# Last keys of the value product in 64-row tiles, one pool of PSUM banks, and engine orders from a table, in an attention kernel with a squared-ReLU feed-forward network

## The chip, the cores and the metric

The kernel runs on one core of one Trainium2 chip. The metric is the device time of one execution in microseconds (us). Engines are written as in the profile: PE is TensorE, DVE is VectorE, ACT is ScalarE, POOL is GpSimd, SP is SyncE; PEld is PE's loading of weights.

## The reference

Eight batches of eight heads, 576 positions, 64 dimensions a head. To the scores a bias is added that depends on the distance of two positions and on the head; then softmax, the product with the values, and a feed-forward network on the 4608 rows of 512:

```python
scores = scale * np.matmul(q, k.transpose(0, 1, 3, 2))
scores = scores + bias.transpose(2, 0, 1)[None, :, :, :]
attn = np.exp(scores - np.max(scores, axis=-1, keepdims=True))
attn = attn / (np.sum(attn, axis=-1, keepdims=True) + 1e-09)
attn_out = np.matmul(attn, v)
x = attn_out.transpose(0, 2, 1, 3).reshape(B * S, H * D)
h = np.maximum(x @ w_in, 0.0)        # w_in 512 x 2048
return h * h @ w_out                 # w_out 2048 x 512
```

## The kernel before, in words

**Attention.** The work goes by pairs of heads, 32 in all (`pair`, L919; four to a batch). Keys are laid on partitions, in four tiles of 128 and a last one of 64 (keys 512 to 575); queries run along the free dimension. Scores of the four full key tiles (`scores_of`, L807, matmul L815) use 64 rows of the array for each head, since a head has 64 dimensions: the two heads of a pair run as two 64-row tiles. They write to a set of two PSUM banks, one bank a head, and one exponential on ACT (L997, 1024 elements a partition) reads the set. The last 64 queries have products of their own (L822, 64 columns each, two banks) and two exponentials (L831, one a head). For the last 64 keys both heads share one full tile (`last_keys`, L1006): `kz` holds head 0's keys on one half of the rows and columns and head 1's on the other, so that one product (L1012) gives both heads' scores on 128 partitions; `pm` holds their exponentials (L1022). The bias enters as a factor: DVE multiplies the bands near the diagonal by a table of exponentials of the bias (L728, the "bands").

The product with the values (`values`, L741) goes over tiles of 128 queries: for each tile one product of the last keys of both heads at once (L754: `pm` against `vm`, which holds zeros where heads don't belong together, 130 columns) and eight of 65 columns (L761: four key tiles for two heads); the 65th column gives the sum of the softmax. A pair is done in two parts, of three and of two query tiles, each in one bank. DVE takes the reciprocal (L775) and writes the normalized rows `x` (L780). From batch 2 on a DMA transpose on SP turns `x` into `xt`, one for each part; for the first two batches PE does it (L1078). The first batch is done in halves of its queries (`half_of_pair`, L840).

**Feed-forward network.** It goes over nine groups of 512 rows, while the attention of later batches runs. The first layer is 16 products of 128 columns of `w_in` for a group (L1501; for group 0 by halves, L1451; part of the groups 2 to 8 by a scheme with seven products for eight, L1378). ACT applies the ReLU (L1530) and DVE squares (L1540) into `g`. The second layer uses seven products for eight as well (L1204), with sums of `g` made on DVE and evictions on DVE and ACT (L1232, L1238).

**Order.** All work is a list of operations with an engine or a choice of engines, what they depend on, and the buffers they take (`Plan.add`). `Plan.schedule` (L191) picks at each step the operation that can start first by a cost model, and among those the one that is due first. Due times come from the code and, for some 500 operations, from a table of numbers (`DUES`, L67). The instructions are then issued in that order, and each engine runs its own in order; semaphores make it wait. A buffer is taken from a ring of slots when the operation is placed. PSUM has two rings: two sets of two banks for scores (`sets_ps`, L347), and four single banks for all else (`g_ps`, L348). The loads of the start are issued by POOL; q and k of a pair go to buffers `qs` and `ks`, the weights in four pieces each.

Of the kernel before, what the change touches and what calls it, by code (L numbers as in the profile page):

```python
# [34 lines left out]
RELU_DVE = 0  # L35
# [31 lines left out]
DUES = """  # L67
# [52 lines left out]
"""  # L120
# [5 lines left out]
class Ring:  # L126


    def __init__(self, n, in_order=False):
        self.free = [(0.0, i) for i in range(n)]  # L130
        self.in_order, self.made, self.taken = in_order, 0, 0


class Buf:


    def __init__(self, ring):
        self.ring, self.left, self.slot, self.until = ring, 0, None, 0.0
        self.turn, ring.made = ring.made, ring.made + 1
# [31 lines left out]
STAY = 0.0  # L171


class Plan:
# [16 lines left out]
    def schedule(self):  # L191
        engines = ("PE", "ACT", "DVE", "POOL", "SP", "DMA", "XB")
        now = {"PE": 600.0, "ACT": 740.0, "DVE": 820.0, "POOL": 1300.0, "SP": 740.0, "DMA": 0.0, "XB": 0.0}
        mode = None
        waiting = {e: [] for e in engines}
        for op in self.ops:
            op.wait = len(op.deps)
            for d in op.deps:
                d.users.append(op)
            if not op.wait:  # L200
                for e in op.engs:
                    waiting[e].append(op)
        done = []
        while len(done) < len(self.ops):
            best = None
            for e in engines:
                pick = None
                for op in waiting[e]:
                    at = max(now[e], op.ready, self._buf_time(op))
                    if at == float("inf"):  # L210
                        continue
                    due = op.due if op.due > -1e8 else op.ready - 1e9
                    if e == "PE" and op.mode != mode:
                        due += STAY
                    key = (max(at, now[e]), due, op.seq)
                    if pick is None or key < pick[0]:
                        pick = (key, op)
                if pick is None:
                    continue
# [50 lines left out]
def act(n):  # L270
    return 174.0 + n / 1.2
# [1337 lines left out]
```

## Time and profile before

| what | us |
|---|---|
| three runs | 360.20, 360.44, 362.07 |
| their median | 360.44 |
| span of the profiled execution, first to last instruction | 358.7 |
| busy: PE, PEld | 346.4, 262.0 |
| busy: DVE, ACT, POOL | 297.5, 272.6, 170.6 |

Of the profiled execution the span is on record and not its time beside it; the median of the runs is 1.7 above the span, for what lies before the first instruction and behind the last. In the profile, a line such as L815 is a line of the kernel before. A row of PE's timeline gives the start, the length of the merged piece, the line, the output and inputs, the tile (128\*128 is the whole array, 64\*128 half of its rows), the shape, and the count. Matmuls are pipelined, so the length of one is longer than the distance between the starts of two.

### The profile page before, as it was taken

Reading aid. Unit: us, or ns where it says so; the run is one execution under the profiler, and the core shown is the slowest. Engines: PE = TensorE matmul, PEld = TensorE weight load, DVE = VectorE, ACT = ScalarE, POOL = GpSimd, SP = SyncE. Lnnn points to the kernel's source line nnn. Section 1 sums busy time; section 2 is a strip of 40 time slices with the busy share of each in tenths; the row PEclk is TensorE's granted clock in tenths of the full one; section 3 lists DMA queues with packets and bytes.
Section 4 is the critical chain, followed back from the end, with each engine's and each line's share of the span. In section 5 each row is a group of like instructions: output and inputs, shape, how many; then the busy total and the mean of one; then the engine's idle time right before and its main releaser. Section 6 shows DMA issues by size and latency. Waiting matters only on the chain.

```text
span 358.7 us, 10742 instructions
## 1 busy us (share of the span) xinstructions
PE 346.4 (97%) x4290; PEld 262.0 (73%) x4290; DVE 297.5 (83%) x673; ACT 272.6 (76%) x435; POOL 170.6 (48%) x289
## 2 busy tenths in 40 slices
PE   3988999999999999999999999999999999999996
PEld 3666788775587558877788568755867887888885
DVE  4888999666996799768896899798988798899993
ACT  4898997589966988678976887689889833899830
POOL 8886679698995896158478456221000000000000
PEclk9999999999999999999999999999999999999999
DMA  9999999999999999799999999863410032010023
GB/s 172 151 147 198 193 150 154 190 156 192 175 130 165 223 158 112 119 163 198 84 134 164 186 126 133 150 121 72 61 44 15 18 97 68 27 63 33 23 66 117
DMA packets 162210, 44.37 MB, mean 124 GB/s; under 512 B 145520, under 2 KB 162160, under 8 KB 162160
## 3 DMA queue, kind: packets, MB, share of 16 engines
q0 software_dynamic: 74208, 14.53, 54.6%
q1 hardware_dynamic: 87696, 28.86, 44.3%
q8 instruction: 33, 0.54, 0.6%
q10 hardware_dynamic: 256, 0.30, 0.3%
q14 instruction: 17, 0.14, 0.1%
HBM read 36.94 MB, written 9.44 MB: 129 GB/s over the span
## 4 chain that ended last, share of the span: by engine, by line
PE 88%; DMA 7%; POOL 2%; ACT 1%; issue 1%; DVE 0%; POOLq 0%
PE f L1204 31%; PE f L1501 20%; PE f L761 10%; PE st L815 8%; PE f L1378 7%; DMA w_in_sb<-in_moe_w_in_dram 5%; PE f L1451 3%; PE st L1378 3%; PE f L754 3%; PE st L1012 2%; DMA ks<-in_k_dram 2%; POOL va L368 2%; PE f L822 1%; PE f L1078 1%; POOL ks L368 0%
## 5 line engine op out<-in xcount | busy, mean ns | idle before, releaser
L997 ACT ACTIVATE pt<-st 128x1024 f16<-128x1024 f32 x112 | 111.1, 1031 | 23.0 <-PE st L815 22.8
L1501 PE MATMUL f<-xt,w_in_sb 128*128 128x512 f16 (+4 forms) x416 | 77.2, 330 | 0.0
L728 DVE TENSOR_TENSOR pt<-pt,tb_sb 128x512 f16<-128x512 f16 (+3 forms) x108 | 61.9, 581 | 12.6 <-ACT pt L997 9.3
L368 POOL DMA_DIRECT2D ks<-in_k_dram x79 | 55.9, 719 | 15.1 <-DMA kt<-ks 10.4
L1204 PEld LDWEIGHTS <-g 128*128 128x128 f16 x576 | 55.1, 98 | 7.6 <-issue 0.8
L368 POOL DMA_DIRECT2D qs<-in_q_dram x79 | 55.5, 712 | 8.1 <-DMA qt<-qs 6.2
L1530 ACT ACTIVATE rt<-f 128x512 f16<-128x512 f32 x80 | 47.3, 608 | 14.1 <-PE f L1501 12.7
L1501 PEld LDWEIGHTS <-w_in_sb 128*128 128x128 f16 x416 | 37.1, 98 | 26.7 <-issue 2.5
L761 PE MATMUL f<-va,pt 128*128 128x65 f16 x1280 | 53.2, 193 | 0.3 <-DMA va<-in_v_dram 0.3
L761 PEld LDWEIGHTS <-pt 128*128 128x128 f16 x1280 | 49.8, 97 | 1.3 <-issue 0.5
L1204 PEld LDWEIGHTS <-s 128*128 128x128 f16 x432 | 41.1, 98 | 5.8 <-issue 0.8
L1232 DVE SCALAR_TENSOR_TENSOR y<-f,y 128x512 f32<-128x512 f32 (+1 forms) x48 | 31.8, 665 | 12.5 <-PE f L1204 11.7
L815 PE MATMUL st<-qt,kt 64*128 64x512 f16 (+1 forms) x288 | 40.4, 361 | 1.0 <-DVE qt L716 0.6
L1540 DVE TENSOR_TENSOR g<-rt 128x512 f16<-128x512 f16 x80 | 34.3, 433 | 6.2 <-ACT rt L1530 5.3
L1204 PE MATMUL f<-wt,g 128*128 128x256 f16 x288 | 35.6, 273 | 0.0
L754 PE MATMUL f<-vm,pm 128*128 128x130 f16 x160 | 35.5, 222 | 0.0
L1204 PE MATMUL f<-w_out_sb,s 128*128 128x256 f16 x288 | 35.3, 273 | 0.0
L1204 PE MATMUL f<-w_out_sb,g 128*128 128x256 f16 x288 | 34.7, 273 | 0.1
L780 DVE TENSOR_TENSOR x<-f,r 128x384 f16<-128x384 f32 (+1 forms) x64 | 30.9, 485 | 0.9
L645 POOL CAST va<-f 128x512 f16<-128x512 f32 x24 | 16.7, 702 | 30.8 <-DMA f<-in_v_dram 17.5
L974 POOL COPY kz<-kt 64x64 f16<-64x64 f16 x55 | 19.4, 354 | 20.2 <-DMA kt<-ks 17.1
L831 ACT ACTIVATE pt<-f 128x256 f16<-128x256 f32 x64 | 22.9, 404 | 5.9 <-PE f L822 4.5
(112 smaller groups left out, 532.4 us busy)
## 6 DMA issues: line engine op xcount, KB each, us to landing
out_dram<-y SPq DMA_DIRECT2D x34, 256.0 KB, 2.8
f<-in_v_dram SPq DMA_DIRECT2D x24, 256.0 KB, 4.9
ks<-in_k_dram POOLq DMA_DIRECT2D x48, 64.0 KB, 5.2
qs<-in_q_dram POOLq DMA_DIRECT2D x48, 64.0 KB, 4.4
w_in_sb<-in_moe_w_in_dram POOLq DMA_DIRECT2D x4, 512.0 KB, 10.7
w_out_sb<-in_moe_w_out_dram POOLq DMA_DIRECT2D x4, 512.0 KB, 8.9
ks<-in_k_dram POOLq DMA_DIRECT2D x7, 144.0 KB, 5.6
qs<-in_q_dram POOLq DMA_DIRECT2D x7, 144.0 KB, 5.5
```

What stands on the lines that cost most here:

```text
L368: lambda: io(eng.dma_start(out=out_(), in_=in_())),
L728: io(nc.vector.tensor_tensor(out=a, in0=a, in1=t, op=MULT))
L754: nc.tensor.matmul(ps[:, i, :, :], pm[:, c : c + 128], vm[:, hp, :, 0:65], start=True, stop=False)
L761: nc.tensor.matmul(ps[:, i, e, :], pt[:, (2 * jt + e) * S + c : (2 * jt + e) * S + c + 128], va[:, jt, 2 * hp + e, 0:65], start=False, sto ...
L815: nc.tensor.matmul(banks[i][:, e, :], kt[rw[e], ts(jt, 128)], qt[rw[e], ds(q0, n)], start=True, stop=True)
L997: nc.scalar.activation(out=p5(pts[pb.slot])[:, jt, :, 0:512], in_=sets_ps[st.slot], func=EXPF, scale=SCALE)
L1204: nc.tensor.matmul(home[bf.slot][:, ts(s_, HALF)], left(c, s_), right(c), start=(c == 0 and (s_ == 0 or apart) and (own or i not in before ...
L1232: nc.vector.scalar_tensor_tensor(out=dst, in0=ps, scalar=OSC, in1=ys[y[plus].slot][:, cs], op0=MULT, op1=mybir.AluOpType.add,)
L1378: nc.tensor.matmul(ps()[:, ds(HALF * f + a, z - a)], left()[:, kk, ts(f, 128)], right(a, z)[:, kk, :], start=(first_ and f == 0 and a == 0 ...
L1501: nc.tensor.matmul(g_ps[bank.slot][:, a:z], w_in_sb[:, kk, ts(nt, 128)], xt_sb[:, kk, c : c + z - a], start=(kk == 0), stop=(kk == 3),)
L1530: io(nc.scalar.activation(out=rts[rb.slot], in_=g_ps[bank.slot], func=RELUF))
L1540: nc.vector.tensor_tensor(out=gs[gb1.slot][:, nt, :], in0=rts[rb.slot], in1=rts[rb.slot], op=MULT)
```

## The change

- **Last keys.** For the 28 pairs of batches 1 to 7 the product with the values is one for the whole pair (`values_of_pair`), with two neighbouring banks, one a head. The last keys are multiplied head by head in 64-row tiles (65 columns each, ten a pair), as an operation of its own that PE can do beside scores; then two operations, one a head, of 20 products of 65 columns. One reciprocal, one norm and one DMA transpose of `x` follow for the pair. The first batch keeps `values`.
- **Banks.** All eight banks are one tile and one ring. An operation takes one bank, or two that are neighbours (`Buf(r_g, 2)`: a run of scores, the last queries, a pair's product).
- **Scores.** Each key tile's scores are an operation of their own; before, they went two by two from batch 1 on. The last queries are one operation with one exponential for both heads.
- **Choices.** In all groups DVE can take a ReLU and ACT a square; before, all but one of these ReLUs were on ACT and all but a part of the squares on DVE.
- **Orders.** The due times go. A table (`TURNS`) holds, for PE, ACT, DVE, POOL and SP, the numbers of the operations in the order in which the engine does them, and with it which engine does what. `Plan.schedule` takes them in that order; only landings of DMAs and the slots of buffers are still found by the model.

The core of the diff:

```diff
-RELU_DVE = 0
+RELU_DVE = 9
-DUES = """
-0:1620 2:1057 4:1180 10:1374 14:10158 16:8662 20:10687 22:11516 35:2669 52:4535 56:9455 58:7112 60:7916 68:10815
+TURNS = {
+    "PE": """
+11 24 18 16 544 14 20 542 550 548 556 570 22 568 554 578 562 566 582 594 560 590 592 575 580 602 606 587 604 631
...
+    def _take(b, start):
+        places = Plan._places(b)
+        if b.ring.banks and b.size == 1:
+            now = {i for t, i in places if t <= start}
+            if now:
+                return min(((i - 1 in now) + (i + 1 in now), i) for i in now)[1]
+        return min(places)[1]
...
-    sets_ps = [psum.tile([128, 2, 512], FP32, name=f"st{i}") for i in range(2)]
-    g_ps = pv_ps = [psum.tile([128, 512], FP32, name=f"f{i}") for i in range(4)]
+    banks_ps = psum.tile([128, 8, 512], FP32, name="bank")
+    g_ps = pv_ps = [banks_ps[:, i, :] for i in range(8)]
-    r_set, r_g, r_lane = Ring(2), Ring(4), Ring(8)
+    r_g, r_lane = Ring(8, banks=True), Ring(8)
...
+    def values_of_pair(p, pb, bands, exps, T, after):
+        st = Buf(r_g, 2)
+        def tails():
+            pm, vm = p4s[pb.slot], v4s[b_v[b].slot]
+            for i in range(5):
+                for e in range(2):
+                    rw = ds(64 * e, 64)
+                    io(
+                        nc.tensor.matmul(
+                            of_head(st, e)[:, ts(i, 65)], pm[rw, ts(i, 128)], vm[rw, hp, e, 0:65],
+                            start=(i == 0), stop=True, skip_group_check=True,
+                        )
+                    )
+        def pv(e):
+            for i in range(5):
+                for jt in range(4):
+                    c = (2 * jt + e) * S + 128 * i
+                    io(
+                        nc.tensor.matmul(
+                            of_head(st, e)[:, ts(i, 65)], pt[:, c : c + 128], va[:, jt, 2 * hp + e, 0:65],
+                            start=False, stop=(jt == 3), skip_group_check=True,
+                        )
+                    )
+        o = P.add({"DVE": 190.0}, recip, made_, [st, rb], T - 2000)
+        o = P.add({"DVE": dve(640)}, norm, [o], [st, rb, xb], T - 2000)
...
-            run([0, 1])
-            last_keys()
-            run([2, 3], True)
+        run(0)
+        run(1)
+        last_keys()
+        run(2)
+        run(3)
+        exps["q"] = last_queries(qb, pb, evac, T, after)
...
-    for op in P.schedule():
+    for op in P.schedule({e: [int(i) for i in x.split()] for e, x in TURNS.items()}):
```

In the kernel after, the lines of the prediction are: scores L954 (before L815), last queries L961 (L822), last keys in 64-row tiles L876 (L754 in the first batch: L826), other keys L892 (L761), scores of the last keys L1149 (L1012), the first layer of group 0 L1578 (L1451), loads L434 (L368).

More of the change, by code (lines that the diff above doesn't have):

```diff
@@ L63, in _bucket, with __init__ @@
     return np.where(n < half, n, large).astype(np.int64)
-DUES = """
[52 rows of a table removed]
-"""
+TURNS = {
+    "PE": """
[27 rows of a table added]
+""",
+    "ACT": """
[17 rows of a table added]
+""",
+    "DVE": """
[26 rows of a table added]
+""",
+    "POOL": """
[11 rows of a table added]
+""",
+    "SP": """
[7 rows of a table added]
+""",
+}
 class Ring:
-    def __init__(self, n, in_order=False):
-        self.free = [(0.0, i) for i in range(n)]
+    def __init__(self, n, in_order=False, banks=False):
+        self.n, self.banks, self.free = n, banks, [(0.0, i) for i in range(n)]
         self.in_order, self.made, self.taken = in_order, 0, 0
 class Buf:
-    def __init__(self, ring):
+    def __init__(self, ring, size=1):
+        self.size = size
         self.ring, self.left, self.slot, self.until = ring, 0, None, 0.0
@@ L189, in land, with schedule @@
         return op
-    def schedule(self):
-        engines = ("PE", "ACT", "DVE", "POOL", "SP", "DMA", "XB")
+    def schedule(self, order):
         now = {"PE": 600.0, "ACT": 740.0, "DVE": 820.0, "POOL": 1300.0, "SP": 740.0, "DMA": 0.0, "XB": 0.0}
         mode = None
-        waiting = {e: [] for e in engines}
+        queues = {e: [self.ops[i] for i in l] for e, l in order.items()}
+        for e, l in queues.items():
+            for op in l:
+                op.engs = {e: op.engs[e]}
+        moves = {e: [] for e in ("DMA", "XB")}
         for op in self.ops:
@@ L227, in schedule @@
                 mode = op.mode
-            for x in op.engs:
-                waiting[x].remove(op)
+            if e in queues:
+                heads[e] += 1
+            else:
+                moves[e].remove(op)
             op.eng, op.start, op.end = e, at, at + took
@@ L233, in schedule @@
                 if b.slot is None:
-                    t, b.slot = min(b.ring.free)
-                    b.ring.free.remove((t, b.slot))
+                    b.slot = self._take(b, op.start)
+                    b.ring.free = [x for x in b.ring.free if not b.slot <= x[1] < b.slot + b.size]
                     b.ring.taken += 1
@@ L239, in schedule @@
                 if not b.left:
-                    b.ring.free.append((b.until, b.slot))
+                    b.ring.free += [(b.until, b.slot + i) for i in range(b.size)]
             for u in op.users:
@@ L247, in schedule @@
                     )
-                    for x in u.engs:
-                        waiting[x].append(u)
+                    if u.fn is None:
+                        moves[next(iter(u.engs))].append(u)
             done.append(op)
@@ L252, in schedule, with _places @@
         return sorted(done, key=lambda o: (o.start, o.seq))
+    @staticmethod
+    def _places(b):
+        if b.size == 1:
+            return b.ring.free
+        at = {i: t for t, i in b.ring.free}
+        return [(max(at[i], at[i + 1]), i) for i in at if i + 1 in at]
+    @staticmethod
+    def _take(b, start):
[5 more added lines that the diff above has]
+        return min(places)[1]
     @staticmethod
@@ L379, in one_of, with squared @@
         return op
+    def squared(o, out_, src):
+        if o.eng == "ACT":
+            io(nc.scalar.activation(out=out_, in_=src, func=SQUAREF))
+        else:
+            io(nc.vector.tensor_tensor(out=out_, in0=src, in1=src, op=MULT))
     def const(f):
@@ L789, in values, with heads, recip, norm @@
         o = P.add({"DVE": dve(nq * 128)}, norm, [o], [bank, rb, xb], T - 2000)
+        return o
+    def values_of_pair(p, pb, bands, exps, T, after):
+        b, hp = divmod(p, 4)
+        xb = x_bufs[p]
+        st = Buf(r_g, 2)
[10 more added lines that the diff above has]
+                    )
+        o = P.add(
+            {"PE": 5 * mm(65) + 3}, tails, [bands["k"]] + l_v[b, hp] + first, [st, pb, b_v[b]], T + 1, after, "r"
+        )
+        def pv(e):
+            pt, va = pts[pb.slot], vas[b_v[b].slot]
+            for i in range(5):
[6 more added lines that the diff above has]
+                        )
+                    )
+        made_ = [
+            P.add(
+                {"PE": 20 * mm(65)}, lambda e=e: pv(e), [o] + list(bands.values()) + list(exps.values()),
+                [st, pb, b_v[b]], T + 1, after, "f",
+            )
+            for e in range(2)
+        ]
+        rb = Buf(r_r)
+        def heads():
+            return in_two(st)[:, :, 0:325].rearrange("p e (t d) -> p e t d", t=5)
+        def recip():
+            io(nc.vector.reciprocal(out=rs[rb.slot], in_=heads()[:, :, :, 64:65]))
+        def norm():
+            io(
+                nc.vector.tensor_tensor(
+                    out=xs[xb.slot].rearrange("p t (e d) -> p e t d", e=2), in0=heads()[:, :, :, 0:64],
+                    in1=rs[rb.slot].to_broadcast([128, 2, 5, 64]), op=MULT,
+                )
+            )
+        o = P.add({"DVE": 190.0}, recip, made_, [st, rb], T - 2000)
+        o = P.add({"DVE": dve(640)}, norm, [o], [st, rb, xb], T - 2000)
@@ L815, in scores_of @@
                     nc.tensor.matmul(
-                        banks[i][:, e, :], kt[rw[e], ts(jt, 128)], qt[rw[e], ds(q0, n)], start=True, stop=True
+                        banks[i][e], kt[rw[e], ts(jt, 128)], qt[rw[e], ds(q0, n)], start=True, stop=True
                     )
@@ L851, in scores @@
         def scores(jt, last=False):
[L852 to L853 removed]
+            st = Buf(r_g, 2)
             def score():
[L856 to L860 removed]
+                banks = [[of_head(st, e)[:, ts(j, 256)] for e in range(2)] for j in range(2)]
+                scores_of(qb.slot, banks, [jt, jt + 1], q0, 256, None)
+            o = P.add({"PE": 2 * mm(256) + 6}, score, evac + ready, [st, qb, pb], T, 0.0, "r")
             def ex():
@@ L1061, in pair @@
             ),
-        ]
+        }
         x_bufs[p] = Buf(r_x)
-        return [
-            values(p, part, qt0, nq, pb, bands + list(exps.values()), T, after) for part, qt0, nq in ((0, 0, 3), (1, 3, 2))
-        ]
+        return values_of_pair(p, pb, bands, exps, T, after)
     def x_turn(b, norms):
```

179 lines of the change are left out of this document (77 added, 102 removed), and 138 rows, old and new, of tables (DUES, TURNS).

## The prediction

> **What bounds the kernel now.** First the page's line of busy times, then the table of who waited for whom with TensorE (PE) as the waiting engine, then the stages.
>
> ```profile
> span 358.7 us, 10742 instructions
> ...
> PE 346.4 (97%) x4290; PEld 262.0 (73%) x4290; DVE 297.5 (83%) x673; ACT 272.6 (76%) x435; POOL 170.6 (48%) x289
> ```
>
> ```profile
> PE f L419 <- DMA id_sb<-c_id: 4.4, 1, 4.4
> PE f L1451 <- DMA w_in_sb<-in_moe_w_in_dram: 1.3, 1, 1.3
> PE f L947 <- ACT ex_sb L424: 1.3, 1, 1.3
> PE st L815 <- DVE qt L716: 0.6, 1, 0.6
> PE f L947 <- DVE qt L716: 0.4, 1, 0.4
> ```
>
> ```profile
> 20.00:34.00 14.00, 11.78 (x238) 8.70 (x234) 11.69 (x35) 13.90 (x27) 10.35 (x25) 1.00 1.33 172
> 34.00:55.00 21.00, 20.67 (x285) 16.56 (x286) 19.86 (x53) 18.49 (x31) 14.78 (x25) 1.00 1.43 176
> 55.00:130.00 75.00, 75.00 (x869) 51.76 (x866) 59.89 (x131) 59.45 (x93) 64.67 (x102) 1.00 1.71 172
> 130.00:250.00 120.00, 119.90 (x1470) 86.83 (x1469) 100.51 (x225) 94.12 (x149) 62.83 (x109) 1.00 1.11 137
> 250.00:300.00 50.00, 50.00 (x675) 39.87 (x674) 44.10 (x108) 35.73 (x57) 0.76 (x3) 1.00 0.25 55
> 300.00:358.70 58.70, 55.55 (x494) 48.01 (x491) 48.26 (x85) 37.23 (x65) 0.00 (x0) 1.00 0.16 52
> ```
>
> A stage row gives its length, then the busy time of PE, PE's weight loads, DVE, ACT and POOL, then the granted clock. From 55 to 300 PE is busy for 244.9 of 245 us at clock 1.00, while DVE has 204.5 and ACT 189.3. All waits of PE that the table names are over by 35 us (the last is the 1.3 us for the second piece of w_in, quoted below). So in the steady part, time goes only if PE has less to do; what ACT and DVE gain or lose there is free until it makes PE wait. Before 34 us it is otherwise: ACT is busy for 13.90 of 14.00 us.
>
> A busy PE is not yet a full one, since its rows overlap. What a matmul costs is the distance from one start to the next. Two pieces of PE's timeline (start, length, line, shape, count) give all the prices:
>
> ```profile
> 149.40 1.92 PE L1204 MATMUL f<-wt,g 128*128 128x256 f16 x16
> 151.15 1.91 PE L1204 MATMUL f<-w_out_sb,s 128*128 128x256 f16 x16
> 153.00 0.60 PE L815 MATMUL st<-qt,kt 64*128 64x512 f16 x4
> 153.44 0.28 PE L822 MATMUL f<-qt,kt 64*128 64x64 f16 x8
> 153.65 1.59 PE L1204 MATMUL f<-wt,g 128*128 128x256 f16 x13
> ```
>
> ```profile
> 133.48 0.23 PE L754 MATMUL f<-vm,pm 128*128 128x130 f16 x1
> 133.55 0.41 PE L761 MATMUL f<-va,pt 128*128 128x65 f16 x8
> ...
> 135.59 0.22 PE L754 MATMUL f<-vm,pm 128*128 128x130 f16 x1
> 135.65 0.40 PE L761 MATMUL f<-va,pt 128*128 128x65 f16 x8
> 135.89 0.65 PE L1012 MATMUL st<-qt,kz 128*128 128x288 f16 x4
> ```
>
> - A product of 256 columns: (151.15 - 149.40) / 16 = 0.109 us.
> - A change between full tiles (128\*128) and 64-row tiles (64\*128): the 16 products from 151.15 should be through at 151.15 + 16 x 0.109 = 152.90, and the scores begin at 153.00, so 0.10 us.
> - Two 64-row tiles of 64 columns: the 8 of L822 with the change behind them take 153.65 - 153.44 = 0.21; less 0.10, four pairs take 0.11 to 0.12, 0.029 a pair. They do run beside each other.
> - A product of the last keys (L754, 130 columns): 135.65 - 135.59 = 0.06. The 8 products of 65 columns (L761) take 135.89 - 135.65 = 0.24, 0.030 each.
>
> **The change part by part.**
>
> *Last keys.* In the 28 pairs of batches 1 to 7, five L754 products go (140 x 0.06 = 8.4 us) and five pairs of 64-row tiles come (140 x 0.029 = 4.1 us). PE has nothing beside these; all of it is on the path: -4.3. Rounding of the starts to 0.01 us makes the first term 7.7 to 9.1. The 1280 products of 65 columns stay.
>
> *Tile changes.* On PE, in the middle of the kernel, a pair's scores and its product with the values read before (L815 scores, L754 last keys, L761 other keys):
>
> ```order
> L815 LDWEIGHTS kt_84
> L815 MATMUL st_116<-qt_80,kt_84 128x512
> L754 LDWEIGHTS pm
> L754 MATMUL f_121<-vm,pm 128x130
> L761 LDWEIGHTS pt
> L761 MATMUL f_121<-va,pt 128x65
> ```
>
> and now (L954 scores, L876 last keys, L892 other keys):
>
> ```order
> L954 LDWEIGHTS kt_85
> L954 MATMUL bank<-qt_81,kt_85 128x512
> L876 LDWEIGHTS pm
> L876 MATMUL bank<-vm,pm 128x65
> L892 LDWEIGHTS pt
> L892 MATMUL bank<-va,pt 128x65
> ```
>
> The last keys have joined the scores' side of the change of tiles. Counted over PE's whole order, PE changes its tiling 154 times before and 159 times now. From the first score of a whole pair (512 columns) on, where PE is the bound, it is 113 and 130: each score run is now placed for itself, and one lone block of last keys costs two changes. 17 x 0.10 = +1.7. The 12 fewer changes ahead of that lie where ACT sets the pace; they are in the next term.
>
> The Trainium skill (TensorEngine Tiling, Key Properties) says that changing the tiling mode drains TensorE, which speaks against putting small products into 64-row tiles at all; the trace agrees, with its 0.10 us. By the rule alone, with 28 blocks of last keys each by itself, 56 changes would eat 5.6 us, more than the 4.3 gained.
>
> *The first 36 us.* POOL issues the loads of the start. Before, between the first and the second piece of w_in stand the second batch's v and a piece of w_out:
>
> ```order
> L368 DMA w_in_sb<-in_moe_w_in_dram 128x4x512
> L368 DMA va<-in_v_dram 128x4x64
> L368 DMA vm<-in_v_dram 64x4x64
> ...
> L368 DMA va<-in_v_dram 128x8x64 x2
> L368 DMA vm<-in_v_dram 64x4x64
> L368 DMA w_out_sb<-in_moe_w_out_dram 128x4x512
> L368 DMA w_in_sb<-in_moe_w_in_dram 128x4x512 x2
> ```
>
> and now two loads stand between them:
>
> ```order
> L434 DMA w_in_sb<-in_moe_w_in_dram 128x4x512
> L434 DMA ks_73<-in_k_dram 96x2x384
> L434 DMA qs_68<-in_q_dram 96x2x384
> L434 DMA w_in_sb<-in_moe_w_in_dram 128x4x512
> L434 DMA w_out_sb<-in_moe_w_out_dram 128x4x512
> ```
>
> ```profile
> 12.89 8.13 DMA w_in_sb<-in_moe_w_in_dram
> 24.42 9.86 DMA w_in_sb<-in_moe_w_in_dram
> ```
>
> Those are the two pieces in the chain that ended last: issued at 12.89 and 24.42, landed at 21.02 and 34.28. The second lay 13.3 us behind the first with 11 loads between them; with two between, a quarter of that is 3 to 4. The first has three more loads of q and k ahead of it now and lands later, by 2 us or so; the second should still be there before 30, and PE's wait of 1.3 us go. What is late next is ACT, full until 34:
>
> ```profile
> L569 ACT ACTIVATE qs<-g 96x768 f16<-96x768 f32 x1 | 0.8, 844 | 0.9 <-DMA g<-in_q_dram 0.9
> L455 ACT ACTIVATE tb_sb<-f 128x512 f16<-128x512 f32 x3 | 1.8, 586 | 0.0
> ```
>
> To there it loses the cast of q (0.84) and one copy of the bias table (0.59), both to DVE, and four joined exponentials save 0.20 each (rows below); it gets one or two squares (0.63 each). That is about 1 us less. So the start gains between 0 and 1.3 + 12 x 0.10 = 2.5; I take 0.8, since ACT's share is what is left to gain.
>
> *ACT and DVE.*
>
> ```profile
> L997 ACT ACTIVATE pt<-st 128x1024 f16<-128x1024 f32 x112 | 111.1, 1031 | 23.0 <-PE st L815 22.8
> L1530 ACT ACTIVATE rt<-f 128x512 f16<-128x512 f32 x80 | 47.3, 608 | 14.1 <-PE f L1501 12.7 <-ACT pm L1022 0.9
> L831 ACT ACTIVATE pt<-f 128x256 f16<-128x256 f32 x64 | 22.9, 404 | 5.9 <-PE f L822 4.5 <-issue 1.2
> L1424 ACT ACTIVATE g<-rt 128x512 f16<-128x512 f16 x32 | 20.0, 630 | 0.9
> L1540 DVE TENSOR_TENSOR g<-rt 128x512 f16<-128x512 f16 x80 | 34.3, 433 | 6.2 <-ACT rt L1530 5.3
> L780 DVE TENSOR_TENSOR x<-f,r 128x384 f16<-128x384 f32 x32 | 17.6, 551 | 0.4
> L780 DVE TENSOR_TENSOR x<-f,r 128x256 f16<-128x256 f32 x32 | 13.4, 419 | 0.6
> L775 DVE RECIPROCAL r<-f 128x6 f32<-128x6 f32 x32 | 6.0, 188 | 3.5 <-PE f L761 3.3
> L775 DVE RECIPROCAL r<-f 128x4 f32<-128x4 f32 x32 | 5.5, 173 | 3.2 <-PE f L761 2.9
> L1464 DVE TENSOR_SCALAR rt<-f 128x512 f16<-128x512 f32 x1 | 0.7, 682 | 0.0
> ```
>
> ACT gives up 35 relus (35 x 0.608 = 21.3) and takes 46 squares (46 x 0.630 = 29.0); 64 exponentials of the last queries become 32 of twice the size (64 x 0.404 = 25.9 against 32 x 0.608 = 19.5, the 512-wide row's price). Net about +1. DVE takes the 35 relus (x 0.682 = 23.9) and gives up 46 squares (x 0.433 = 19.9); 28 pairs have one reciprocal (about 0.21) and one norm of 640 elements (0.551 + 2 x (0.551 - 0.419) = 0.815) for two of each: 28 x (0.188 + 0.173 + 0.551 + 0.419 - 0.21 - 0.815) = 8.6 less. Net about -5, less four evictions of y that moved to it (+2.7). Both stay below 85% of the span; the cover is PE's own work, and I cost this at nothing by itself. SP issues one transpose of x for two (24 less, none of them waited for by PE before).
>
> *Waits.* All eight banks are one pool, and a pair's product holds two neighbouring ones from its first last-keys product to its norm. Behind a PE instruction that waits for a bank stands all of PE's queue. The table of waits of before names none after 35 us, so the nearest rows bound it: nothing below, and above, one exponential (1.03) at each of 28 pairs, 29 us. An order that keeps most of PE's work between an exponential and the next use of its bank is nearer the first; I take +0.5 and keep up to +3 for the forecast's range. Below nothing it can't go, since no such wait is there to be gained.
>
> Sum: -8.4 + 4.1 + 1.7 - 0.8 + 0.5 = -2.9. The profiled execution's span is 358.7, and the median of the runs lies 1.7 above it (360.44); the span becomes 355.8 and the time **357.5**. With the terms' ends (-9.1 or -7.7; -2.5 or 0; 0 or +3) the forecast's own range is 354.6 to 361.5, mostly 355.5 to 359.
>
> **The rivals.**
>
> - *Pairs of banks run short (slower).* A score run, the last queries and a product each need two neighbouring free banks, where before the scores had two sets of their own. If PE waits for one, everything stands. Beyond the 0.5 taken, 0.10 us a pair (2.9 / 28) eats the gain and 0.17 (4.7 / 28) makes a loss that can be measured; at 0.25 it is 28 x 0.25 = 7, 364.5. For it: ACT had 76% of the span and a run's bank pair is free only 1.03 us after its scores. Against: the table names no wait of PE for an exponential after 35 us in the old pools, where the scores had four banks and now may take any two of eight. The Trainium skill's page on tiling (TensorEngine Tiling, Gotcha 1: PSUM Pressure) says that row tiles must write to different banks and so raise the need for them; no run here shows yet what that costs.
> - *ACT's queue (no change).* 46 squares now stand between exponentials. If one square of 0.63 holds up an exponential that PE needs in one pair in seven, 28 / 7 x 0.63 = 2.5 are lost: 360.0. For it: ACT's row of L997 waits 22.8 us for scores in all, so it has slack, but not evenly. Against: 35 relus left the same queue.
> - *The 64-row tiles don't overlap (no change).* Then 280 x 0.029 = 8.1 replace 8.4: 357.5 + 4.1 = 361.6. Against: the 8 products of L822 in 0.12 us.
> - *The start gives all (faster).* Wait for w_in and changes of tiles gone, no new waits: 357.5 - 1.7 - 0.5 = 355.3.
>
> **How the numbers follow.** A measurement of this kernel can tell about 0.5% from no change, 1.8 us: faster is below 358.6, slower above 362.2. The forecast gets 0.53, the start 0.17, ACT's queue 0.14, the tiles 0.05, the banks 0.11. Of the forecast's range a small part is above 358.6, so faster has 0.53 - 0.03 + 0.17 = 0.67, same 0.14 + 0.05 + 0.03 - 0.01 = 0.21, slower 0.11 + 0.01 = 0.12 (a hundredth of the tiles' case lies over the line). The range takes the start's case below and the two "no change" cases above and leaves out the banks: 354.3 to 361.6.
>
> **What would show it.** In the profile after: PE's starts 0.029 apart for each pair of L876, and no 0.06 between tiles in L892; changes of 0.10; PE without named waits after 36 us; no wait for w_in of over 0.3 at L1578; L954 or L876 waiting for ACT or DVE is the banks' case. The prediction is wrong if PE's busy time from 55 to 300 falls below 99%, or if the time is above 361.6 or below 354.3.

## The result, and the profile after

The changed kernel takes 355.14 us in the median of four runs (354.42 to 356.06), against 360.40 before, where a fourth run has joined the three above: 0.984 of the time, 95% interval 0.981 to 0.988. Measured again later, it took 356.11 (355.48 to 356.46) beside 360.58 for the kernel before: 0.989, 0.986 to 0.991. So it is faster by 4.5 to 5.3 us; the forecast was 2.9. Of the kernel before's 75 runs beside the experiments 23 had a granted clock of about 0.995 and took 361.1 to 361.2 us in the median, against 359.5 to 360.0 for the others; no run of the kernel after had it, so against the others alone the second measurement's gain is 3.4.

The page of the kernel after, its span and busy times:

```profile
span 353.4 us, 10852 instructions
...
PE 343.8 (97%) x4430; PEld 258.1 (73%) x4430; DVE 299.1 (85%) x620; ACT 273.4 (77%) x409; POOL 168.0 (48%) x281
```

The span is 5.3 shorter, like the median; both profiled executions had a granted clock of 1.00. The table of who waited for whom, PE's rows (total, times, longest):

```profile
PE bank L491 <- DMA id_sb<-c_id: 3.0, 1, 3.0
PE bank L515 <- DMA g<-c_oh: 0.8, 1, 0.8
PE bank L954 <- DVE kt L788: 0.5, 1, 0.5
PE bank L1021 <- ACT pt L1006: 0.5, 1, 0.5
PE bank L1089 <- ACT ks L641: 0.5, 1, 0.5
PE bank L876 <- ACT pt L1136: 0.2, 1, 0.2
```

The wait for the second piece of w_in (1.3 us before) is gone. One wait is new in the steady part, at L876, the last keys, for an exponential; the profile of the second measurement doesn't have it. The stages (length, then busy time of PE, its weight loads, DVE, ACT, POOL, then the granted clock):

```profile
0.00:20.00 20.00, 14.15 (x303) 10.84 (x304) 14.71 (x50) 14.96 (x24) 17.56 (x30) 1.00 1.23 156
20.00:34.00 14.00, 13.89 (x294) 11.17 (x294) 12.98 (x45) 14.00 (x23) 8.36 (x15) 1.00 1.25 203
34.00:55.00 21.00, 20.90 (x302) 16.53 (x295) 20.19 (x49) 19.25 (x30) 14.81 (x25) 1.00 1.69 180
55.00:130.00 75.00, 74.76 (x877) 49.52 (x874) 64.01 (x123) 58.95 (x83) 60.83 (x101) 1.00 1.51 171
130.00:250.00 120.00, 119.88 (x1575) 86.72 (x1574) 100.32 (x195) 97.46 (x141) 65.54 (x111) 1.00 1.04 136
```

From 20 to 34 us PE was busy for 11.78 before and is busy for 13.89 now, with ACT full in both. From 55 to 130 it is busy for 74.76 of 75, where it had been busy throughout (as it is in the second measurement). PE's timeline in the steady part (start, length, line, tile, count) has the prices of the last keys:

```profile
134.76 0.39 PE L954 MATMUL bank<-qt,kt 64*128 64x512 f16 x2
134.99 0.28 PE L961 MATMUL bank<-qt,kt 64*128 64x64 f16 x8
135.10 0.32 PE L876 MATMUL bank<-vm,pm 64*128 64x65 f16 x10
135.35 1.39 PE L892 MATMUL bank<-va,pt 128*128 128x65 f16 x40
136.57 0.41 PE L1149 MATMUL bank<-qt,kz 128*128 128x288 f16 x2
```

Four pairs of 64 columns take 135.10 - 134.99 = 0.11, 0.028 a pair; ten tiles of last keys with the change behind them take 0.25, five pairs of 0.030 and 0.10; the 40 products of L892 take 1.22, 0.0305 each, with nothing between query tiles. No tile change stands between the last queries and the last keys: that is the order's doing.

**Where the 5.3 us come from.** PE's own work can be added up from such distances over its whole order, a tile change at 0.096 (its median in the trace): 343.3 us before, with 154 changes, and 340.0 after, with 159. What an execution takes beyond that sum is put down to waiting. The table gives it, up to the point where that much of the work has been started:

| beyond PE's own work, us | before | after | after, second measurement |
|---|---|---|---|
| at the first matmul | 4.4 | 3.0 | 3.0 |
| at 10 us of work | 7.3 | 5.7 | 6.9 |
| at 36 us of work | 9.2 | 6.0 | 7.1 |
| at 200 | 11.1 | 8.6 | 9.4 |
| at the last matmul | 12.1 | 10.1 | 10.9 |

The sum is an estimate, and so are the entries: with other prices from the same traces (the mean distance of each full-tile shape, the median of each pair of small tiles) it is 343.2 and 339.6, and the entries from 10 us of work on are 0.1 to 3.4 us larger. The differences between the columns hold better: from before to after, the waiting at 36 us of work then shrinks by 3.2 (2.0 in the second measurement) and grows by 1.5 (1.1) from there to the end. Only at 10 us of work do they change (0.8 and 0.0 in place of 1.6 and 0.4), and that row is not read. Only one execution of the kernel before has a profile.

The work itself is 3.3 shorter: 3.9 for the last keys and 1.1 for fewer early changes, less 1.6 for more changes in the steady part. Up to 36 us of work the waiting shrinks by 3.2 (2.1 in the second measurement), and from there to the end it grows by 1.2 (0.9). 3.9 - 1.6 + 1.1 + 3.2 - 1.2 = 5.4, within rounding of 5.3. The two measurements of the same kernel differ by 1.0 us in the time and by 1.1 at 36 us of work: the first microseconds, which wait for loads, do not come out alike each time. A difference of under 1 us in the start is therefore not read as an effect below.

ACT's timeline shows what else changed in the start. ACT began the first of the sixteen half-pair exponentials of the first batch at 10.84 before and at 10.67 after (10.91 in the second measurement), and the last at 33.42 and 30.37 (31.52). From the one start to the other it takes 22.58 us before and 19.70 (20.61) after. Of these it is idle for 0.80 before and 0.04 (0.75) after, and busy for 21.78 and 19.66 (19.85). So some 2 us of the difference are work that no longer stands between these exponentials; idle time adds 0.8 in one execution and nothing in the other. ACT's timeline before, with the rows that stand between (in brackets idle time and what ended it):

```profile
10.84 1.94 ACT L864 ACTIVATE pt<-st 128x1024 f16<-128x1024 f32 x2
13.47 0.65 ACT L714 ACTIVATE qt<-f 128x576 f16<-128x576 f16 x1 [0.70 <-PE f L947]
14.02 0.59 ACT L455 ACTIVATE tb_sb<-f 128x512 f16<-128x512 f32 x1
...
30.40 0.69 ACT L714 ACTIVATE kt<-f 128x576 f16<-128x576 f16 x1
...
32.89 0.66 ACT L1022 ACTIVATE pm<-st 128x576 f16<-128x576 f32 x1
33.42 1.04 ACT L864 ACTIVATE pt<-st 128x1024 f16<-128x1024 f32 x1
```

and after:

```profile
7.09 0.65 ACT L786 ACTIVATE kt<-bank 128x576 f16<-128x576 f16 x1 [0.30 <-PE bank L1089]
...
8.68 0.65 ACT L786 ACTIVATE qt<-bank 128x576 f16<-128x576 f16 x1 [0.45 <-PE bank L1089]
9.23 0.65 ACT L786 ACTIVATE kt<-bank 128x576 f16<-128x576 f16 x1
10.12 0.65 ACT L786 ACTIVATE kt<-bank 128x576 f16<-128x576 f16 x1 [0.25 <-PE bank L1089]
10.67 1.02 ACT L1006 ACTIVATE pt<-bank 128x1024 f16<-128x1024 f32 x1
...
30.37 1.09 ACT L1006 ACTIVATE pt<-bank 128x1024 f16<-128x1024 f32 x1
...
32.70 0.73 ACT L1159 ACTIVATE pm<-bank 128x576 f16<-128x576 f32 x1
```

Before, two copies of the turned q and k out of PSUM (0.55 and 0.53 us from start to start), a copy of the bias table (0.48) and the last keys' exponential of the next batch (0.53) stand between the first and the last of the sixteen: 2.1 us. After, the four copies of q and k that ACT makes up to there all stand ahead of the first exponential, which yet begins no later: the cast of q (0.75) has gone to DVE, and ACT is idle there for 0.4 to 0.6 us less. One copy of the table has gone to DVE too, and the next batch's exponential stands behind the last. The joined exponentials take 0.2 less, and a square (0.54) has come.

The last of the sixteen ends at 34.46 before, 31.46 after and 32.58 in the second measurement, and PE's waiting at 36 us of work (9.2, 6.0, 7.1 in the table) lies 25.3 to 25.5 below these times. With the other prices, this distance is 21.4 to 22.4 in all thirteen profiles that have eight banks, while the end itself goes from 31.4 to 35.7. The two move together, as they would if ACT set the pace up to there.

### The profile page after: what moved, and what is told of

It is laid out like the page before. It is cut to its first block, busy times and chain, and to the rows that moved or that the text cites. A ratio compares the mean times of both kernels' runs of the same rounds, so it can differ in the third digit from the quotient of the medians.

```text
span 353.4 us, 10852 instructions
## 1 busy us (share of the span) xinstructions
PE 343.8 (97%) x4430; PEld 258.1 (73%) x4430; DVE 299.1 (85%) x620; ACT 273.4 (77%) x409; POOL 168.0 (48%) x281
## 4 chain that ended last, share of the span: by engine, by line
PE 87%; ACT 7%; DVE 4%; DMA 1%; issue 1%; ACTq 0%
PE bank L1335 30%; PE bank L1626 17%; PE bank L1505 10%; PE bank L892 9%; PE bank L954 8%; PE bank L1578 4%; ACT pt L1006 2%; PE bank L1149 2%; PE bank L876 1%; PE bank L1089 1%; DMA g<-in_k_dram 1%; ACT rt L1655 1%; PE bank L961 1%; DVE s L1290 1%; PE bank L833 1%; ACT pt L1136 1%
## 5 line engine op out<-in xcount | busy, mean ns | idle before, releaser
L1136 ACT ACTIVATE pt<-bank 128x1024 f16<-128x1024 f32 x112 | 110.2, 1032 | 12.1 <-PE bank L954 10.9
L1626 PE MATMUL bank<-xt,w_in_sb 128*128 128x512 f16 (+4 forms) x416 | 77.7, 330 | 0.1
L434 POOL DMA_DIRECT2D qs<-in_q_dram x79 | 55.8, 714 | 13.1 <-DMA qt<-qs 8.8
L434 POOL DMA_DIRECT2D ks<-in_k_dram x79 | 55.9, 713 | 5.9 <-DMA kt<-ks 2.8
L954 PE MATMUL bank<-qt,kt 64*128 64x512 f16 (+1 forms) x288 | 42.6, 358 | 1.0 <-DVE kt L788 0.5
L1363 DVE SCALAR_TENSOR_TENSOR y<-bank,y 128x512 f32<-128x512 f32 (+1 forms) x48 | 31.9, 664 | 10.6 <-PE bank L1335 10.2
L892 PE MATMUL bank<-va,pt 128*128 128x65 f16 x1120 | 39.6, 193 | 0.0
L892 PEld LDWEIGHTS <-pt 128*128 128x128 f16 x1120 | 36.7, 97 | 3.3 <-issue 2.0
L1655 ACT ACTIVATE rt<-bank 128x512 f16<-128x512 f32 x49 | 28.6, 596 | 10.5 <-PE bank L1626 10.3
L1335 PE MATMUL bank<-w_out_sb,s 128*128 128x256 f16 x288 | 36.4, 273 | 0.0
L1335 PE MATMUL bank<-wt,g 128*128 128x256 f16 x288 | 36.3, 273 | 0.0
L1335 PE MATMUL bank<-w_out_sb,g 128*128 128x256 f16 x288 | 35.2, 273 | 0.0
L449 ACT ACTIVATE g<-rt 128x512 f16<-128x512 f16 x45 | 28.4, 635 | 2.8 <-DVE rt L1657 2.0
```

Source lines behind the costliest of these rows:

```text
L434: lambda: io(eng.dma_start(out=out_(), in_=in_())),
L449: io(nc.scalar.activation(out=out_, in_=src, func=SQUAREF))
L892: nc.tensor.matmul(of_head(st, e)[:, ts(i, 65)], pt[:, c : c + 128], va[:, jt, 2 * hp + e, 0:65], start=False, stop=(jt == 3), skip_group_ ...
L954: nc.tensor.matmul(banks[i][e], kt[rw[e], ts(jt, 128)], qt[rw[e], ds(q0, n)], start=True, stop=True)
L1136: nc.scalar.activation(out=p5(pts[pb.slot])[:, jt, :, 0:512], in_=in_two(st), func=EXPF, scale=SCALE)
L1335: nc.tensor.matmul(home[bf.slot][:, ts(s_, HALF)], left(c, s_), right(c), start=(c == 0 and (s_ == 0 or apart) and (own or i not in before ...
```

## The experiments

The theory (**sum**): the gain is the prediction's sum, PE's own work with each tile change paid, and the rest came in the start. Against it stood **cover** or **start** theories (the last keys, the changes or the loads cost nothing because something else ends later), then several causes for the start. Times are medians; the kernel before took 360.32 beside the first four, 359.84 beside the next four and 360.58 beside the last four.

**Last keys as full tiles.** Ten full-height products in place of ten 64-row tiles; the order is kept.

```diff
-                    rw = ds(64 * e, 64)
...
-                            of_head(st, e)[:, ts(i, 65)], pm[rw, ts(i, 128)], vm[rw, hp, e, 0:65],
+                            of_head(st, e)[:, ts(i, 65)], pm[:, ts(i, 128)], vm[:, hp, e, 0:65],
```

> The changed kernel with the last keys of each pair in ten products over all 128 rows (the zeros of vm take the other head's part away) in place of ten in 64-row tiles; the place in the order is the same. Sum theory (what PE has to do is all that counts in the steady part): a pair's ten products take 0.30 us in place of 0.147, 28 x 0.153 = 4.3 more, and PE changes its tiling 167 times in place of 159, 0.8 more: 355.1 + 5.1 = 360.2. Start theory (the 5.3 us came from the start, the tiles brought little): no more than 1 us, 356.

360.82 (359.33 to 362.45), 1.000 of before (0.998 to 1.002): the whole gain is gone. PE's timeline of this kernel shows why:

```profile
137.73 0.28 PE L960 MATMUL bank<-qt,kt 64*128 64x64 f16 x8
137.94 0.48 PE L875 MATMUL bank<-vm,pm 128*128 128x65 f16 x10
138.26 1.37 PE L891 MATMUL bank<-va,pt 128*128 128x65 f16 x40
```

The ten now take 138.26 - 137.94 = 0.32, the change has moved ahead of them (0.21 from L960 to L875, with 0.11 of work), and the five overlapped pairs of 0.030 would have been 0.15. That is 0.17 a pair of heads (0.16 to 0.18 with the rounding of the starts), 28 x 0.17 = 4.8, and eight more changes of tiling over the whole order are 0.8: 5.6, against 4.7 to 5.7 measured. The overlap of two 64-row tiles is paid in full on the path.

**Lone blocks of last keys.** In 12 pairs of heads PE's order has the ten tiles between products of full tiles instead of behind scores: 183 changes for 159. For that one product of full tiles is moved ahead of them; nothing else changes.

```diff
 L954 MATMUL bank<-qt_80,kt_84 128x512
-L876 MATMUL bank<-vm,pm 128x65
...
+L1335 MATMUL bank<-wt,g_100 128x256
...
+L876 MATMUL bank<-vm,pm 128x65
```

> The changed kernel with PE's order altered at 12 pairs: a neighbouring full-array product is moved between the scores and the last keys, so that the 64-row block of the last keys stands alone. 24 more changes of tiling, nothing else added. Sum theory: 24 x 0.096 = 2.3 and a few tenths where the moved product is early or late: 357.4 to 358.0. Cover theory (a change of tiling costs only while nothing else holds PE up): under 1 us, below 356.1.

358.37 (357.64 to 359.51), 0.994 of before: 2.3 to 3.2 above the changed kernel, and 24 x 0.096 = 2.3. Its profile also has a wait of 0.9 for the first piece of w_in, at 24.41 and so ahead of the first moved product (64.67): a start that the edit doesn't touch can differ by that much. One of the twelve in its timeline:

```profile
64.67 1.05 PE L1335 MATMUL bank<-wt,g 128*128 128x256 f16 x8
65.65 0.33 PE L876 MATMUL bank<-vm,pm 64*128 64x65 f16 x10
65.91 1.05 PE L1335 MATMUL bank<-w_out_sb,s 128*128 128x256 f16 x8
```

Eight products of 0.109 are 0.87 and take 0.98: 0.10 is the first change; the ten tiles take 0.26, 0.15 and a second 0.10. Each change costs its 0.10 here, where PE is the bound. The Trainium skill's sentence that changing the tiling mode drains TensorE (TensorEngine Tiling, Key Properties) agrees, and 0.10 us is what it costs here.

**Loads late.** POOL issues the second batch's v and a piece of w_out ahead of the second piece of w_in again, as in the kernel before.

```diff
 L434 DMA qs_68<-in_q_dram 96x2x384
-L434 DMA w_in_sb<-in_moe_w_in_dram 128x4x512
-L434 DMA w_out_sb<-in_moe_w_out_dram 128x4x512
+L434 DMA va<-in_v_dram 128x8x64
+L434 DMA vm<-in_v_dram 64x4x64
+L434 DMA w_out_sb<-in_moe_w_out_dram 128x4x512
+L434 DMA w_in_sb<-in_moe_w_in_dram 128x4x512
 L434 DMA qs_72<-in_q_dram 96x2x384
```

> The changed kernel with POOL's loads of the start put back in one point: the second batch's first v, its last keys' v and the first piece of w_out are loaded ahead of the second piece of w_in, which then lands at about 32.5 in place of 27.3. PE comes to it at about 29. Sum theory (PE's waits of the start are carried to the end one for one): 3 to 4 us more, 358 to 359. Cover theory (ACT is full until 34 anyway, so a wait of PE there is hidden): at most 1 us, below 356.1.

358.61 (357.9 to 361.94), 0.997 of before: 2.5 to 3.5 lost, and carried to the end. Its waits and its stage from 20 to 34:

```profile
PE bank L1578 <- DMA w_in_sb<-in_moe_w_in_dram: 1.5, 1, 1.5
```

```profile
20.00:34.00 14.00, 12.34 (x240) 9.29 (x240) 11.71 (x41) 12.59 (x21) 7.96 (x14) 1.00 1.34 200
```

PE waits 1.5 for w_in and ACT is idle for 1.4 of the 14 us; what else makes up the 2.5 to 3.5 has no wait of its own in the table. The early second piece is needed.

**The one-hot table before the identity.** SP's first two loads in the old kernel's order.

```diff
+L434 DMA g_100<-c_oh 128x512
 L434 DMA id_sb<-c_id 128x416
-L434 DMA g_100<-c_oh 128x512
```

> The changed kernel with SP's first two loads in the old order, the one-hot table before the identity, so that the first matmul starts at 4.3 in place of 3.0. Sum theory: 1.3 more, 356.4. Cover theory: the scores wait for k, whose load lands at 5.4 and which ACT casts after that, so that little of it is left: 0 to 0.5, 355.1 to 355.6.

355.61 (355.2 to 357.42), 0.987 of before: within the two measurements of the changed kernel. Which of the two comes first is worth nothing that can be seen.

**The old choices of engine.** All plain ReLUs on ACT and all their squares on DVE again, with the order searched anew for that (173 changes for 159).

> The changed kernel with the choice of engines put back: all ReLUs of the first layer's plain products on ACT, all their squares on DVE, as before the change (36 ReLUs and 45 squares move). The table of orders was searched anew around these moves; it has 173 changes of tiling in place of 159. Sum theory (ACT and DVE have room, the choices are worth nothing by themselves): 14 x 0.096 = 1.3 more, 356.5. Waits theory (the choices are what keeps PE fed in the steady part): PE's busy share from 55 to 300 falls below 99% and the time is above 358.

358.98 (358.11 to 360.91), 0.998 of before: 2.9 to 3.8 slower than the change, of which 14 x 0.096 = 1.3 are changes. PE was busy for 244.14 of 245 us from 55 to 300, so it stands between the two theories: some waits, fewer than the waits theory had. Since the order differs throughout, it doesn't say what the choices are worth by themselves.

**The kernel before with the second piece of w_in earlier,** its orders held by a table; in the second run the identity goes first on SP too.

```diff
 L435 DMA ks_71<-in_k_dram 96x2x384
+L435 DMA w_in_sb<-in_moe_w_in_dram 128x4x512
 L435 DMA va<-in_v_dram 128x8x64 x2
 L435 DMA vm<-in_v_dram 64x4x64
 L435 DMA w_out_sb<-in_moe_w_out_dram 128x4x512
-L435 DMA w_in_sb<-in_moe_w_in_dram 128x4x512
```

> The kernel before, all orders held as they were, with one load of POOL moved: the second piece of w_in ahead of the second batch's v and the first piece of w_out, so that it lands at about 30 in place of 34.3. Sum theory: PE's wait of 1.3 us goes and is carried to the end, 360.4 - 1.3 = 359.1. Cover theory: ACT, full until 34, is late next and nothing or little is gained, 360.0 to 360.4. If the loads that now come later are waited for, it is slower.

> As the run with w_in moved in the kernel before, and SP's first two loads exchanged as well, the identity first, so that the first matmul starts at 3.0 in place of 4.4. Sum theory: 360.4 - 1.3 - 1.3 = 357.8. By the run in which the exchange was undone in the changed kernel (0.5): 358.6. Cover theory: 360.

360.61 (359.56 to 363.02), 1.002 of before (0.999 to 1.004), and 360.89, 1.002: no gain. The waits of the first of them no longer name w_in:

```profile
PE f L486 <- DMA id_sb<-c_id: 4.2, 1, 4.2
PE f L1014 <- ACT ex_sb L491: 1.3, 1, 1.3
PE f L828 <- DMA va<-in_v_dram: 0.7, 1, 0.7
```

and ACT's last half-pair exponential begins where it did (33.42 before):

```profile
33.68 1.04 ACT L931 ACTIVATE pt<-st 128x1024 f16<-128x1024 f32 x1
```

In the old structure the wait of 1.3 us for w_in hid behind ACT: without it PE is no further at 36 us of its work (9.4 beyond it, 9.2 before). Together with the late loads this says that the early w_in is needed in the new kernel and doesn't give the gain by itself.

**Seven banks.** One bank is taken from the pool; the orders stay.

```diff
+    r_g.free = r_g.free[:7]
```

> The changed kernel with seven banks in the pool in place of eight, all orders held. If the pool has room (the forecast's view of the banks), a few waits of under 1 us, 355 to 358. Banks theory (the order uses the pool to the last bank, and a missing one stops PE at most pairs by about one exponential, 1.03): 28 x 1.03 = 29 us or more, above 380.

390.72 (389.43 to 391.42), 1.084 of before. Its waits and its steady part:

```profile
PE bank L955 <- ACT pt L1137: 6.3, 8, 1.1
PE bank L877 <- ACT pt L1137: 4.9, 5, 1.1
PE bank L1336 <- ACT pt L1137: 2.1, 4, 0.8
PE bank L962 <- ACT pt L1137: 2.0, 2, 1.1
```

```profile
55.00:300.00 245.00, 224.38 (x2783) 156.19 (x2782) 185.90 (x358) 176.53 (x246) 127.43 (x214) 1.00 0.97 123
```

PE loses 20.6 of 245 us to waits of up to 1.1, one exponential long, at scores (L955), last keys (L877) and second-layer products. The pool has no spare bank for this order, which was found for eight. The Trainium skill says that row tiles raise the need for PSUM banks (TensorEngine Tiling, Gotcha 1: PSUM Pressure); this run shows that the need is the whole pool, not that the row tiles alone make it so.

**The changed kernel again,** as the yardstick of the next three:

> The changed kernel as it is, as the yardstick beside the other three: 355.1 (354.4 to 356.1).

356.11 (355.48 to 356.46); its numbers are in the table above.

**Scores of the first batch in three fixed sets of banks.** The order of the start is searched anew.

```diff
-            st = Buf(r_g, 2)
+            st = Buf(r_g, 2, range(6))
...
+        return [(max(at[i], at[i + 1]), i) for i in at if i + 1 in at and (b.among is None or i % 2 == 0)]
```

> The changed kernel, but in the first batch the scores of a half-pair may take only three fixed sets of two banks (banks 0 and 1, 2 and 3, 4 and 5), and the order of the first part is searched anew for that; the old kernel had two such sets. Pool theory (the start gained 3.2 us beside its fewer tile changes because any two neighbouring free banks can take scores, so that ACT finds the next scores ready): part of the 3.2 is lost, 1 us or more, 356.1 to 358.3, and the half-pair exponentials have gaps between them again. Rival (the order alone, or the moved loads and copies): within 0.5 of the changed kernel, 354.7 to 355.6.

357.39 (356.71 to 360.15), 0.993 of before: 1.3 above the yardstick, inside the pool theory's band. But its timeline of ACT gives another cause:

```profile
1.64 1.28 ACT L496 ACT_TABLE_LOAD   x1 [1.64 <-PEq L1711]
...
6.53 1.28 ACT L476 ACT_TABLE_LOAD   x1
7.83 1.08 ACT L527 ACTIVATE tb_sb<-bank 128x512 f16<-128x512 f32 x2
...
11.67 1.02 ACT L1006 ACTIVATE pt<-bank 128x1024 f16<-128x1024 f32 x1 [0.19 <-PE bank L954]
13.20 4.68 ACT L1006 ACTIVATE pt<-bank 128x1024 f16<-128x1024 f32 x5
...
31.89 1.15 ACT L1006 ACTIVATE pt<-bank 128x1024 f16<-128x1024 f32 x1
```

The search put the exponential of L496 ahead of the explicit load of ACT's table (L476), and ACT loaded a table twice: 1.28 us more on ACT before the first exponential. From the first to the last of the sixteen this kernel takes 33.04 - 11.67 = 21.4 us, against 20.8 and 21.7 in the two profiles of the changed kernel. The gaps that the pool theory had forecast are not there (0.5 us of idle time between the first and the last start, within the 0.04 and 0.75 of the changed kernel), so free choice of banks in the first batch, beyond three sets, is not what made that run denser. The band was met for another reason.

**The kernel before, its start searched anew.**

> The kernel before with its two sets and four single banks, its orders held by a table and the part up to 45 us searched anew for the best order. Order theory (any good order of the start gives the gain): about 3 us faster than before, 357. Structure theory (the gain needs the one pool, the joined exponentials and the separate key tiles): 0 to 0.6 faster, 359.8 to 360.4.

361.14 (358.81 to 362.46), 1.001 of before (0.999 to 1.004). In its profile the sixteen exponentials take 24.0 us from first to last, as long as in the kernel before (23.6), with ACT waiting for scores for 1.6 of it. Two copies of the turned q and k (1.2 us) still stand between them. (The granted clock of this profile was 0.98 and 0.90 in the first two stages.) This order did not give the gain. It was one order, so this doesn't show that none could.

**The last queries' exponential split again,** one a head, in the changed kernel.

```diff
-            io(
-                nc.scalar.activation(
-                    out=p5(pts[pb.slot])[:, :, :, 512:S].rearrange("p j e s -> p e j s"),
...
+            for e in range(2):
+                io(
+                    nc.scalar.activation(
+                        out=p5(pts[pb.slot])[:, :, e, 512:S],
```

> The changed kernel with the last queries' exponential of a pair split again into one a head (256 elements each, as before); all else and the orders as they are. If ACT sets the pace of the start and has slack behind it: 4 pairs of the first batch at 2 x 0.404 - 0.608 = 0.20 us, 0.8 slower, 355.9. If ACT's work is nowhere on the path: 355.1. If ACT is near the bound in the steady part too: 28 pairs more at 0.20, up to 5.6 slower, 360.7.

356.55 (356.18 to 356.85), 0.4 above the yardstick, between two of the cases and within what two measurements of one kernel differ by. The sixteen exponentials take 21.0 us. ACT's timeline tells why so little changes; first this kernel, then the changed one:

```profile
19.99 0.79 ACT L977 ACTIVATE pt<-bank 128x256 f16<-128x256 f32 x2
20.51 1.18 ACT L1007 ACTIVATE pt<-bank 128x1024 f16<-128x1024 f32 x1
```

```profile
19.45 0.72 ACT L976 ACTIVATE pt<-bank 128x512 f16<-128x512 f32 x1
19.95 1.14 ACT L1006 ACTIVATE pt<-bank 128x1024 f16<-128x1024 f32 x1
```

Two of 256 elements occupy ACT for 0.52 from start to start, one of 512 for 0.50. The join saves 0.02 here, and at most 0.05 in the other pairs of the first batch, not the 0.20 that the rows' lengths gave.

## Why the prediction came out as it did

The direction was right, by the reasons given, and the time lies in the range; the forecast was short by 1.6 to 2.4 us. One term, the start, was short by 2.4 to 3.5, and the last keys and the waits took back 0.8 to 1.1. By the steps:

- *Last keys, -4.3.* Measured -3.9 in PE's own work; full tiles instead give 4.7 to 5.7 back. The pairs cost 0.028 to 0.030, as read from L822. The removed products had been put at 0.06, from starts rounded to 0.01; their median distance in the trace is 0.057: 140 x 0.003 = 0.4.
- *Tile changes, +1.7.* 17 x 0.096 = 1.6, and the lone blocks showed that each change is on the path. Putting the last keys beside scores is what keeps the rule against mode changes from eating the gain.
- *The first 36 us, -0.8.* The term that was mis-sized: "I take 0.8, since ACT's share is what is left to gain". Measured 3.2 less waiting, 2.1 in the second measurement, and 1.1 for changes of tiles that no longer happen: 3.2 to 4.3. The bound of 2.5 was too low as well. That ACT sets the pace there fits the profiles, and without it the early w_in brings nothing. What was wrong was ACT's share of "about 1 us". It was worked out from the instructions that ACT gives up or joins, with the stage from 20 to 34 (13.90 of 14.00 busy) for proof that nothing else could go. But what counts is what stands between the sixteen exponentials. Two copies of q and k moved ahead of them and one exponential of the next batch behind them: 1.6 us that ACT still does, out of the way. One term of that work was itself too large: four joined exponentials, at 0.20, save 0.02 to 0.05 each.
- *w_in.* The second piece is there in time, as forecast, and must be (late loads: 2.5 to 3.5 us). The 1.3 us of its old wait were no gain in themselves.
- *Waits, +0.5.* Measured 0.9 to 1.2 from 36 us of work to the end, in many small pieces, of which the table names 0.2 at L876 in one of the two profiles. Within the bounds that were kept (0 to 3).
- *ACT and DVE at nothing.* PE was busy for 244.6 of 245 us from 55 to 300, so their changed loads cost no more than the waits above. DVE's load itself rose by 1.6 (297.5 to 299.1), where the rows had given 2 less.
- *The rivals.* Pairs of banks did not run short in this order, but the reason given against it was half wrong: scores "may take any two of eight" didn't mean room, since seven banks cost 35 us. ACT's queue and tiles that don't overlap are refuted by the stages and by the full tiles. *The start gives all* came nearest in time, 355.3, by its sign; its sum (no new waits, start at 2.5) is not what happened, so that its number fits is chance.

**What stays open:** ACT's denser run is read from the traces; no run changed it alone. Whether the new structure is needed to clear the sixteen exponentials of other work, or a better order of the old kernel would do, isn't shown: the one searched order of the old kernel left two copies and 1.6 us of waiting for scores between them. The identity's place, the joined exponentials and the free choice of banks beyond three sets are each not needed, as far as 1 us can be told, and the early w_in isn't enough. Two sets, as in the old pools, against three was not tried in the new kernel.

## What to carry to other kernels

Where an engine looks full in one stage, look at what stands in its queue between the instructions that others wait for: work that can go ahead of them or behind them holds them up, and moving it shortens the stage with no work removed. A small product that holds zeros in half of its rows is worth splitting into two row tiles when PE is the bound and it can stand beside work in the same tiling; count the changes of tiling over the whole order, each at its measured price. And before an experiment's time is taken for its theory, look in its profile for a second cause of the same size.

## What the runs showed of the hardware

- Two 64-row tiles of 64 or 65 columns run beside each other at 0.028 to 0.030 us a pair, the price of one full-height product of 65 columns (0.0305); a change between tilings costs 0.10.
- ACT's rows overlap like PE's: 0.39 to 0.40 of length for an exponential of 256 elements, but 0.26 from one to the next. A sum of lengths overstates what a joined instruction saves.
- An activation that stands ahead of the explicit load of ACT's table brings a load of its own, 1.28 us, and the explicit one still follows with another 1.28.
- Two profiled executions of the same kernel differ by 1.1 us in the end of the first batch's last half-pair exponential (31.46 and 32.58); PE's wait for the load of `c_oh` was 0.8 and 1.3.
